# LayerNorm statistics and norms of a chunk: moved from the output stages into K and GLU work

## The chip, the cores and the metric

The kernel runs on one core of one Trainium2 chip. The metric is the device time of one execution in microseconds (us); of several executions the median is given.

## What is computed

The input x has 2048 rows of 640. It is normalised by row and goes through sliding-window attention (32 heads of 20, window 256). A gated unit (GLU) works on the same rows beside it, and x itself is the residual. The core of the reference:

```python
x = A_x
xn = _layernorm(x, axis=-1)
return x + _A_ref(xn, A_wqkv, A_wo) + _B_ref(xn, B_w_gate, B_w_up, B_w_down)

# _A_ref: q, k, v = split(xn @ wqkv); softmax over the last 256 keys; o @ wo
# _B_ref: h = _sigmoid(xn @ w_gate) * (xn @ w_up); h @ w_down
# _layernorm: (x - mean) / sqrt(var + 1e-5)
```

So both branches read the same normalised xn. (B_x is passed in but not used.)

## The kernel before

**Tiling.** The 2048 rows are four chunks of 512 (c = 0 to 3), each of four blocks of 128 rows (s = 0 to 3). Every chunk goes through these stages: LayerNorm with a transpose of the result (xnT, features on partitions), the projections Q and K (`g_qk`, ten blocks of five matmuls), V (`g_v`), the gate and up products of the GLU (`g_gu`, twelve f with a gate half and an up half each), attention, and the output stage (`g_out`: for each block of rows the down product, then Wo into the same PSUM, then the residual).

**LayerNorm of a block.** `ln_block` puts two statistics instructions (L195) and an aggregate (L197) on VectorE (DVE), then two tiny instructions on GpSimd (POOL, L199 and L200), which make rstd out of the variance. `norm_block` (L205) is one DVE instruction that waits for that rstd. `transpose_block` does five TensorE (PE) transposes into one PSUM slot (L213) and one copy out of it into xnT, by DVE for chunks 1 to 3 (L218).

**Attention.** A group is four heads. `scores` (L382) does one step of a group: PE scores (L388), two exps on ScalarE (ACT, L394) and mask selects on POOL (L399, L403). Each group has three steps. `pv` (L407) multiplies a group's probabilities by V (L414), one step into the next group, and DVE finishes the group (L424 to L434).

**The order of the work.** The program order is written out by hand (`manual_schedule`), and every engine works through its queue in that order. The attention steps are the frame (L523). Between two steps `Fill` issues other work: it holds a list of labelled parts (L499 to L513), each a Python generator that issues some instructions and yields their PE cost in ns. After each step a credit, proportional to the step's width, is spent by pulling from the first part. An output stage is shut until its chunk's attention is done (L522, L532). `mix(a, b, first)` (L469) runs generator a and, from its item number `first` on, pulls one item of b after each item of a.

**Where LayerNorm stands.** Chunk 0 is normalised at the start. LN(1) is mixed into the GLU of chunk 0 from item 8 on ("gu0"), LN(2) into output stage 0 from item 6 on ("out0"), LN(3) into output stage 1 from item 6 on ("out1"). `g_ln` (L269) issues for each s the statistics of block s, the norm of block s-1, and the transposes of block s-2; each is an item of its own.

**Buffers that matter.** One PSUM pool, ps_d, has three slots, shared by the projections, gate and up, the two halves of y in the output stage, and the LayerNorm transposes. A gate slot is freed by the tanh on ACT (L316), an up slot by h on DVE (L324), a Q slot by a DVE cast (L238), a K slot by an ACT cast (L240), a V slot by DVE (L264), the y slots by the residual adds on DVE (L357). The tanh results have two buffers (tp), the probabilities four (pp), the normalised blocks xn four.

Of the kernel before, what the change touches and what calls it, by code (L numbers as in the profile page):

```python
# [18 lines left out]
SBC = CW // P  # L19
# [51 lines left out]
def kernel(  # L71
# [119 lines left out]
    def ln_block(c, s):  # L191
        xs = xc[c][:, s, :]
        stats = lnp.tile([P, 2, nc.vector.BN_STATS_DIM], FP32, name="stats")
        for a in range(2):
            nc.vector.bn_stats(out=stats[:, a, :], in_=xs[:, a * 320:(a + 1) * 320])  # L195
        mv = lnp.tile([P, nc.vector.BN_AGGR_DIM], FP32, name="mv")
        nc.vector.bn_aggr(out=mv, in_=stats)  # L197
        rstd = lnp.tile([P, 1], FP32, name="rstd")
        nc.gpsimd.tensor_scalar(out=rstd, in0=mv[:, 1:2], scalar1=EPS, scalar2=None, op0=ADD)  # L199
        nc.gpsimd.tensor_tensor(out=rstd, in0=rstd, in1=neghalf, op=POW)  # L200
        return mv, rstd

    def norm_block(c, s, mv, rstd):
        xn = lnp.tile([P, D], BF16, name="xn", bufs=4)
        nc.vector.tensor_scalar(out=xn, in0=xc[c][:, s, :], scalar1=mv[:, 0:1],  # L205
                                scalar2=rstd[:, 0:1], op0=SUB, op1=MULT)
        xns[c, s] = xn

    def transpose_block(c, s, act):
        xn = xns.pop((c, s))  # L210
        pt = ps_d.tile([P, DC, P], BF16, name="pt", tag="d")
        for d in range(DC):
            nc.tensor.transpose(pt[:, d, :], xn[:, d * P:(d + 1) * P], ident)  # L213
        dst = xnT[c][:, :, s * P:(s + 1) * P]
        if act:
            nc.scalar.copy(out=dst, in_=pt)
        else:
            nc.vector.tensor_copy(out=dst, in_=pt)  # L218

    def new_xnT(c):  # L220
        xnT[c] = xtp.tile([P, DC, CW], BF16, name="xnT")
# [5 lines left out]
    def proj_block(w, c, m):  # L227


        base = 0 if w == "q" else D  # L230
        ps = ps_d.tile([P, CW], FP32, name="pqk", tag="d")
        for d in range(DC):
            wt = wqkv[:, d, base:base + D].rearrange("p (k m) -> p m k", m=DC)
            nc.tensor.matmul(ps, lhsT=wt[:, m, :], rhs=xnT[c][:, d, :],  # L234
                             start=(d == 0), stop=(d == DC - 1))
        st = stp.tile([P, CW], BF16, name="st")
        if w == "q":
            nc.vector.tensor_copy(out=st, in_=ps)  # L238
        else:
            nc.scalar.copy(out=st, in_=ps)  # L240
        dst = scratch[w, c % 2].rearrange("(h j) s -> h j s", j=32)
        nc.sync.dma_start(out=dst[:, 4 * m:4 * m + 4, :], in_=st)

    def spread(w, c, g0, g1):

        if g0 == 0:
            qk[w, c] = (qp if w == "q" else kp).tile([P, NG, CW], BF16, name=w + "T")
        src = scratch[w, c % 2].rearrange("(g p) s -> p g s", p=P)
        nc.sync.dma_start(out=qk[w, c][:, g0:g1, :], in_=src[:, g0:g1, :])
# [16 lines left out]

    MM = 216

    def g_ln(c):  # L269

        new_xnT(c)
        stat = {}
        for s in range(SBC + 2):
            if s < SBC:
                stat[s] = ln_block(c, s)
                yield 0
            if 0 <= s - 1 < SBC:
                norm_block(c, s - 1, *stat[s - 1])
                yield 0
            if 0 <= s - 2:  # L280
                transpose_block(c, s - 2, False)
                yield 5 * 64

    def g_qk(c):
        for w in "qk":
            for m in range(DC):
                proj_block(w, c, m)
                if w == "k" and m == 1:
                    spread("q", c, 0, NG)
                yield 5 * MM  # L290
        if c == 0:
            spread("k", c, 0, 1)
            spread("k", c, 1, NG)

    def g_v(c):
        for s in range(SBC):
            proj_v(c, s)
            if s == 0:
                spread("k", c, 0, NG)
            yield 10 * 136  # L300
# [4 lines left out]
    def part(w, d, f):  # L305
        k, first = divmod(f * P, FS)
        return w[k][:, d, first:first + P]

    def g_gu(c, f0, f1):
        for f in range(f0, f1):  # L310
            pg = ps_d.tile([P, CW], FP32, name="pg", tag="d")
            for d in range(DC):
                nc.tensor.matmul(pg, lhsT=part(wg, d, f), rhs=xnT[c][:, d, :],  # L313
                                 start=(d == 0), stop=(d == DC - 1))
            th = tp.tile([P, CW], FP32, name="th")
            nc.scalar.activation(out=th, in_=pg, func=TANH, scale=0.5)  # L316
            yield 5 * MM
            pu = ps_d.tile([P, CW], FP32, name="pu", tag="d")
            for d in range(DC):
                nc.tensor.matmul(pu, lhsT=part(wu, d, f), rhs=xnT[c][:, d, :],  # L320
                                 start=(d == 0), stop=(d == DC - 1))
            h = hp.tile([P, CW], BF16, name="h")
            ht[c, f] = h
            nc.vector.scalar_tensor_tensor(out=h, in0=th, scalar=1.0, in1=pu, op0=ADD, op1=MULT)  # L324
            yield 5 * MM
# [4 lines left out]
    def out_psum(kind):  # L330
        if kind == "s":
            t = ps_s.tile([P, 2, CW], FP32, name="y", tag="s")
            return [t[:, 0, 0:HALF], t[:, 1, 0:HALF]]
        return [ps_d.tile([P, CW], FP32, name=f"y{i}", tag="d")[:, 0:HALF] for i in range(2)]

    def down(c, s, ys):
        for hf in range(2):
            for f in range(FC):
                nc.tensor.matmul(ys[hf], lhsT=ht[c, f][:, s * P:(s + 1) * P],  # L339
                                 rhs=wd[:, f, hf * HALF:(hf + 1) * HALF],  # L340
                                 start=(f == 0), stop=False)
                if f == 5:
                    yield 6 * 136
            yield 6 * 136

    def outp(c, s, ys, last=False):
        sb = c * SBC + s
        y = yp.tile([P, D], BF16, name="y_sb")

        def wo_half(hf):  # L350
            for m in range(DC):
                nc.tensor.matmul(ys[hf], lhsT=oc[c, m][:, s * P:(s + 1) * P],  # L352
                                 rhs=wo[:, m, hf * HALF:(hf + 1) * HALF],
                                 start=False, stop=(m == DC - 1))

        def add_half(hf):
            nc.vector.scalar_tensor_tensor(  # L357
                out=y[:, hf * HALF:(hf + 1) * HALF], in0=ys[hf], scalar=0.5,
                in1=xc[c][:, s, hf * HALF:(hf + 1) * HALF], op0=MULT, op1=ADD)

        if last:
            for hf in range(2):
                wo_half(hf)
                add_half(hf)
                cut = slice(hf * HALF, (hf + 1) * HALF)
                (nc.scalar, nc.sync)[hf].dma_start(out=out2[sb * P:(sb + 1) * P, cut], in_=y[:, cut])
        else:
            wo_half(0)
            wo_half(1)
            add_half(0)  # L370
            add_half(1)
            nc.sync.dma_start(out=out2[sb * P:(sb + 1) * P, :], in_=y)
        yield 10 * 136

    def g_out(c):
        for s in range(SBC):
            ys = out_psum("d")
            yield from down(c, s, ys)
            yield from outp(c, s, ys)
# [86 lines left out]
            while label not in self.done and self.parts:  # L466
                self.one()

    def mix(a, b, first):  # L469

        for k, cost in enumerate(a):
            yield cost
            if k >= first:
                yield next(b, 0)
        for cost in b:
            yield cost

    new_xnT(0)
    stat = {0: ln_block(0, 0)}
# [12 lines left out]
    fill = Fill()  # L492
    GU = 10 * MM
    OUT = 4 * 34 * 136
    def later(c):
        load_x(c)
        yield 0

    fill.add("gu0", mix(g_gu(0, 0, 12), g_ln(1), 8), 12 * GU + 1280)  # L499
    fill.add("qk1", g_qk(1), 50 * MM)  # L500
    fill.add("v1", g_v(1), 40 * 136)
    fill.add("gu1a", g_gu(1, 0, 1), 1 * GU)
    fill.add("out0", mix(g_out(0), g_ln(2), 6), OUT + 1280)
    fill.add("x3", later(3), 0)
    fill.add("qk2", g_qk(2), 50 * MM)
    fill.add("v2", g_v(2), 40 * 136)
    fill.add("gu1b", g_gu(1, 1, 12), 11 * GU)
    fill.add("out1", mix(g_out(1), g_ln(3), 6), OUT + 1280)
    fill.add("qk3", g_qk(3), 50 * MM)
    fill.add("v3", g_v(3), 40 * 136)  # L510
    fill.add("gu2", g_gu(2, 0, 12), 12 * GU)
# [27 lines left out]
    c = NCH - 1  # L539
# [46 lines left out]
```

## Time and profile before

| what | value |
|---|---|
| median of 13 executions | 341.14 us (339.21 to 343.83) |
| the profiled execution, own time | 340.45 us |
| its span, first to last instruction | 338.6 us |
| mean TensorE clock granted | 0.995 |
| PE, DVE, ACT, POOL busy | 94%, 48%, 64%, 49% of the span |
| share of PE on the chain that ended last | 83% |
| DMA | 30.89 MB, mean 91 GB/s |

Where the stages lie in the span, by the instructions' start times: GLU of chunk 0 with LN(1) from 34 to 67 us, Q and K of chunk 1 from 67 to 83, V of chunk 1 from 83 to 92, output stage 0 with LN(2) from 96 to 121, Q, K and V of chunk 2 from 121 to 143, GLU of chunk 1 from 143 to 173, output stage 1 with LN(3) from 173 to 203.

How to read the profile: the page first gives each engine's busy time, its share of the span and its number of instructions. Then the span is cut into 40 slices of 8.5 us; a digit is the busy share in tenths, and PEclk the granted TensorE clock in tenths. A line of waits says which engine and line waited for which, then the total in us, how many times, and the longest. A table by stretch has the stretch, its length, for PE, its weight loads, DVE, ACT and POOL the busy us with the number of instructions, then the clock, the DMA share and GB/s. A line in order of time has the start, the length (both us), engine, line, operation, and what it writes and reads.

### The profile page before, as it was taken

The page shows a single profiled execution, that of the slowest core. Times are in us where ns is not written, and L with a number is a line of the kernel's source. Part 1 is how long each engine was busy: PE and PEld are TensorE (multiplying, and loading weights), DVE is VectorE, ACT ScalarE, POOL GpSimd, SP SyncE. Part 2 cuts the span into 40 slices and gives each one's busy share as a digit, 9 for nine tenths or more (in the row PEclk, how much of TensorE's full clock was granted, in tenths as well). Part 3 has the DMA queues.
Part 4 walks back from the last instruction along what each step waited for, and adds up shares of the span by engine and source line. Part 5 has one row for each costly group of instructions (what it writes and reads, how often), then busy time and mean ns, then how long its engine had stood idle before and what let it go on. Part 6 is the DMA issues. An engine that isn't in the chain of part 4 may idle for free.

```text
span 338.6 us, 7191 instructions
## 1 busy us (share of the span) xinstructions
PE 318.7 (94%) x2855; PEld 165.8 (49%) x2884; DVE 162.9 (48%) x333; ACT 218.2 (64%) x274; POOL 165.3 (49%) x312
## 2 busy tenths in 40 slices
PE   5999978989899999999999899999999999999996
PEld 2654423435456655544455554544445664444664
DVE  4332079572646853734445846364443434444142
ACT  2623775869675668788874636878787666887300
POOL 5200447554557745564545755545545455554300
PEclk9999999999999999999999979999999999999999
DMA  8947997124600144610000002540000010000002
GB/s 270 376 156 195 360 390 226 38 77 124 205 0 22 41 128 114 221 42 3 0 2 21 19 21 83 181 162 2 2 0 3 21 40 20 2 0 2 2 10 68
DMA packets 26224, 30.89 MB, mean 91 GB/s; under 512 B 1456, under 2 KB 25648, under 8 KB 26160
## 3 DMA queue, kind: packets, MB, share of 16 engines
q1 hardware_dynamic: 25904, 30.20, 27.2%
q8 instruction: 22, 0.36, 0.5%
q10 hardware_dynamic: 288, 0.25, 0.2%
q14 instruction: 10, 0.08, 0.1%
HBM read 21.00 MB, written 10.26 MB: 92 GB/s over the span
## 4 chain that ended last, share of the span: by engine, by line
PE 83%; DVE 6%; ACT 4%; DMA 4%; issue 2%; POOL 1%; SPq 0%; ACTq 0%; POOLq 0%
PE pg L313 14%; PE pu L320 14%; PE y L339 13%; PE pqk L234 13%; PE ps L388 9%; PE acc L414 6%; PE pv L260 6%; PE y L352 6%; ACT pT L394 3%; DMA xc<-in_A_x_dram 2%; DMA sk<-st 1%; DVE stats L195 1%; PE pt L213 1%; DVE t L424 1%; DVE on L430 1%
## 5 line engine op out<-in xcount | busy, mean ns | idle before, releaser
L394 ACT ACTIVATE pT<-ps 128x1024 bf16<-128x1024 f32 (+2 forms) x192 | 175.9, 971 | 66.5 <-PE ps L388 65.0
L399 POOL TENSOR_SCALAR_AFFINE_SELECT pT<-pT 128x512 bf16<-128x512 bf16 x128 | 81.6, 638 | 80.4 <-ACT pT L394 80.4
L403 POOL TENSOR_SCALAR_AFFINE_SELECT pT<-pT 128x512 bf16<-128x512 bf16 x112 | 71.9, 642 | 58.7 <-ACT pT L394 58.7
L324 DVE SCALAR_TENSOR_TENSOR h<-th,pu 128x512 bf16<-128x512 f32 x48 | 32.8, 684 | 62.3 <-ACT pT L394 24.4
L320 PE MATMUL pu<-xnT,wu 128*128 128x512 bf16 x231 | 58.0, 380 | 2.2 <-issue 1.0
L313 PE MATMUL pg<-xnT,wg 128*128 128x512 bf16 x228 | 59.2, 380 | 0.8
L339 PE MATMUL y<-wd,h 128*128 128x320 bf16 x384 | 58.4, 303 | 1.3 <-DVE y_sb L357 1.3
L234 PE MATMUL pqk<-xnT,wqkv 128*128 128x512 bf16 x192 | 45.8, 382 | 0.5 <-issue 0.2
L339 PEld LDWEIGHTS <-h 128*128 128x128 bf16 x384 | 36.1, 99 | 18.6 <-issue 5.4
L388 PE MATMUL ps<-qT,kT 20*128 20x384 bf16 (+2 forms) x704 | 39.6, 277 | 4.2 <-ACT pT L394 3.1
L424 DVE STREAM_TRANSPOSE t<-acc 128x512 f32<-128x512 f32 x32 | 22.9, 715 | 33.0 <-PE acc L414 32.7
L316 ACT ACTIVATE th<-pg 128x512 f32<-128x512 f32 x48 | 28.8, 600 | 14.1 <-PE pg L313 12.3
L313 PEld LDWEIGHTS <-wg 128*128 128x128 bf16 x240 | 22.1, 98 | 27.0 <-issue 3.2
L320 PEld LDWEIGHTS <-wu 128*128 128x128 bf16 x240 | 21.4, 98 | 28.2 <-issue 6.5
L234 PEld LDWEIGHTS <-wqkv 128*128 128x128 bf16 x200 | 22.3, 119 | 19.3 <-issue 2.9
L388 PEld LDWEIGHTS <-kT 20*128 20x128 bf16 x704 | 12.3, 92 | 35.7 <-issue 34.0
L357 DVE SCALAR_TENSOR_TENSOR y_sb<-y,xc 128x320 bf16<-128x320 f32 x32 | 15.1, 488 | 27.0 <-PE y L352 26.9
L414 PE MATMUL acc<-pT,v 128*32 128x384 bf16 (+2 forms) x704 | 26.0, 277 | 1.9 <-POOL pT L403 1.4
L260 PE MATMUL pv<-wqkv,xnT 128*128 128x320 bf16 x160 | 23.9, 299 | 0.4 <-DVE v L264 0.4
L352 PE MATMUL y<-wo,oc 128*128 128x320 bf16 x160 | 24.1, 299 | 0.0
L414 PEld LDWEIGHTS <-v 128*32 128x32 bf16 x704 | 15.1, 96 | 15.4 <-issue 12.5
L238 DVE CAST st<-pqk 128x512 bf16<-128x512 f32 x20 | 13.8, 691 | 13.7 <-PE pqk L234 12.0
(32 smaller groups left out, 175.1 us busy)
## 6 DMA issues: line engine op xcount, KB each, us to landing
qT<-sq SPq DMA_DIRECT2D x4, 1024.0 KB, 5.9
kT<-sk SPq DMA_DIRECT2D x3, 1024.0 KB, 5.5
sq<-st SPq DMA_DIRECT2D x20, 128.0 KB, 2.1
sk<-st SPq DMA_DIRECT2D x20, 128.0 KB, 2.8
wqkv<-in_A_wqkv_dram SPq DMA_DIRECT2D x3, 800.0 KB, 6.8
out_dram<-y_sb SPq DMA_DIRECT2D x15, 160.0 KB, 1.8
wg<-in_B_w_gate_dram SPq DMA_DIRECT2D x2, 960.0 KB
wu<-in_B_w_up_dram SPq DMA_DIRECT2D x2, 960.0 KB
```

The costliest lines, as they stand in the source:

```text
L234: nc.tensor.matmul(ps, lhsT=wt[:, m, :], rhs=xnT[c][:, d, :], start=(d == 0), stop=(d == DC - 1))
L260: nc.tensor.matmul(ps[:, 0:HALF], lhsT=xnT[c][:, d, s * P:(s + 1) * P], rhs=wqkv[:, d, 2 * D + hf * HALF:2 * D + (hf + 1) * HALF], start=( ...
L313: nc.tensor.matmul(pg, lhsT=part(wg, d, f), rhs=xnT[c][:, d, :], start=(d == 0), stop=(d == DC - 1))
L320: nc.tensor.matmul(pu, lhsT=part(wu, d, f), rhs=xnT[c][:, d, :], start=(d == 0), stop=(d == DC - 1))
L324: nc.vector.scalar_tensor_tensor(out=h, in0=th, scalar=1.0, in1=pu, op0=ADD, op1=MULT)
L339: nc.tensor.matmul(ys[hf], lhsT=ht[c, f][:, s * P:(s + 1) * P], rhs=wd[:, f, hf * HALF:(hf + 1) * HALF], start=(f == 0), stop=False)
L352: nc.tensor.matmul(ys[hf], lhsT=oc[c, m][:, s * P:(s + 1) * P], rhs=wo[:, m, hf * HALF:(hf + 1) * HALF], start=False, stop=(m == DC - 1))
L388: nc.tensor.matmul(pss[i // 2][:, i % 2, col * P:(col + n) * P], lhsT=qk["k", kc][32 * i:32 * i + DH, g, kb * P:(kb + 1) * P], rhs=qk["q", ...
L394: nc.scalar.activation(out=pt[:, 2 * a:2 * a + 2, 0:width * P], in_=pss[a][:, :, 0:width * P], func=EXP, scale=SCALE)
L399: nc.gpsimd.affine_select(out=v, in_=v, pattern=[[0, HG], [1, P]], compare_op=GE, fill=0.0, base=0, channel_multiplier=-1)
L403: nc.gpsimd.affine_select(out=v, in_=v, pattern=[[0, HG], [-1, P]], compare_op=GE, fill=0.0, base=-1, channel_multiplier=1)
L414: nc.tensor.matmul(acc[32 * i:32 * i + 32, q0 * P:(q0 + n) * P], lhsT=v[:, h * VW:h * VW + 32], rhs=pt[:, i, col * P:(col + n) * P], start ...
```

## The change

`g_ln` is split in two. `g_norms` keeps statistics and norms; the norm of block s-2 is now issued after the statistics of block s, where it was s-1. `g_transposes` has the transposes alone. `chain` runs generators one after the other, and `mix` gets a parameter `every`, so that b is pulled only at every so-many-th item of a.

For chunk 1 all stays in the GLU of chunk 0, one item later, and all transposes come after all norms. For chunk 2 the statistics and norms go into Q and K of chunk 1, from item 2 on; for chunk 3 into the GLU of chunk 1, from item 10 on. Output stages 0 and 1 keep only the transposes, at items 1, 4, 7 and 10. The costs told to `Fill` stay the same.

```diff
-    def g_ln(c):
+    def g_norms(c):
 
         new_xnT(c)
         stat = {}
@@
             if s < SBC:
                 stat[s] = ln_block(c, s)
                 yield 0
-            if 0 <= s - 1 < SBC:
-                norm_block(c, s - 1, *stat[s - 1])
+            if s >= 2:
+                norm_block(c, s - 2, *stat[s - 2])
                 yield 0
-            if 0 <= s - 2:
-                transpose_block(c, s - 2, False)
-                yield 5 * 64
+
+    def g_transposes(c):
+        for s in range(SBC):
+            transpose_block(c, s, False)
+            yield 5 * 64
+
+    def chain(*gens):
+        for g in gens:
+            yield from g
@@
-    def mix(a, b, first):
+    def mix(a, b, first, every=1):
 
         for k, cost in enumerate(a):
             yield cost
-            if k >= first:
+            if k >= first and (k - first) % every == 0:
                 yield next(b, 0)
@@
-    fill.add("gu0", mix(g_gu(0, 0, 12), g_ln(1), 8), 12 * GU + 1280)
-    fill.add("qk1", g_qk(1), 50 * MM)
+    fill.add("gu0", mix(g_gu(0, 0, 12), chain(g_norms(1), g_transposes(1)), 9), 12 * GU + 1280)
+    fill.add("qk1", mix(g_qk(1), g_norms(2), 2), 50 * MM)
@@
-    fill.add("out0", mix(g_out(0), g_ln(2), 6), OUT + 1280)
+    fill.add("out0", mix(g_out(0), g_transposes(2), 1, 3), OUT + 1280)
@@
-    fill.add("gu1b", g_gu(1, 1, 12), 11 * GU)
-    fill.add("out1", mix(g_out(1), g_ln(3), 6), OUT + 1280)
+    fill.add("gu1b", mix(g_gu(1, 1, 12), g_norms(3), 10), 11 * GU)
+    fill.add("out1", mix(g_out(1), g_transposes(3), 1, 3), OUT + 1280)
```

## The prediction

> **What bounds the kernel now.** I read the page first: engine totals, then the slices.
>
> ```profile
> PE 318.7 (94%) x2855; PEld 165.8 (49%) x2884; DVE 162.9 (48%) x333; ACT 218.2 (64%) x274; POOL 165.3 (49%) x312
> ...
> PE   5999978989899999999999899999999999999996
> ...
> PEclk9999999999999999999999979999999999999999
> ```
>
> TensorE is busy in 318.7 of 338.6 us; no other engine passes 64%. The change leaves PE's work alone, so it can win only PE idle time (19.9 us, head and tail included) and slow PE time (the 7 in PEclk, a slice of 8.5 us). So I asked for busy time by stretch: LN(1) waiting and catching up, the rest of GLU chunk 0, the stage out0, the stage out1, and a short stretch inside out1.
>
> ```profile
> 42.00:54.00 12.00, 7.82 (x72) 3.20 (x65) 9.06 (x23) 6.92 (x10) 6.70 (x13) 1.00 0.95 348
> 54.00:68.00 14.00, 13.84 (x124) 6.25 (x124) 9.59 (x19) 11.63 (x18) 8.74 (x16) 1.00 0.39 106
> ...
> 94.00:122.00 28.00, 27.41 (x298) 17.00 (x297) 18.18 (x41) 17.61 (x19) 19.03 (x35) 1.00 0.05 19
> ...
> 174.00:203.00 29.00, 26.76 (x288) 16.40 (x285) 14.94 (x37) 15.87 (x17) 16.73 (x30) 0.94 0.05 18
> 195.00:199.00 4.00, 3.98 (x26) 2.13 (x26) 1.12 (x3) 1.94 (x2) 2.19 (x4) 0.57 0.12 41
> ```
>
> The first number after the length is PE's busy time. PE misses 4.2 us in 42-54, 0.2 in 54-68, 0.6 in out0, 2.2 in out1; and in 195-199 its clock is 0.57. Then the waits of PE in out1, and DVE in order of time just before.
>
> ```profile
> PE y L339 <- DVE y_sb L357: 1.3, 1, 1.3
> PE pt L213 <- DVE xnT L218: 0.6, 1, 0.6
> PE ps L388 <- ACT pT L394: 0.2, 1, 0.2
> ```
>
> ```profile
> 192.74 0.48 DVE L218 COPY xnT<-pt 128x640 bf16<-128x640 bf16 x1
> 193.14 0.87 DVE L195 BATCH_NORM_STATS2 stats<-xc 128x6 f32<-128x320 bf16 x2
> 194.05 0.21 DVE L197 BATCH_NORM_AGGREGATE mv<-stats 128x2 f32<-128x12 f32 x1
> 194.17 0.39 DVE L205 TENSOR_SCALAR xn<-xc,mv,rstd 128x640 bf16<-128x640 bf16 x1
> 194.48 0.88 DVE L357 SCALAR_TENSOR_TENSOR y_sb<-y,xc 128x320 bf16<-128x320 f32 x2
> ```
>
> The residual adds (L357) that free the next block's PSUM stand behind a copy, statistics and a norm on DVE. Wo had ended at about 192.2; the adds start at 194.48, so down (L339) starts at 195.02.
>
> For GLU chunk 0 the waits of PE in 42-68 read:
>
> ```profile
> PE acc L414 <- POOL pT L403: 1.4, 1, 1.4
> PE ps L388 <- ACT pT L394: 1.1, 2, 0.6
> PE pu L320 <- DVE h L324: 0.8, 1, 0.8
> ```
>
> The cause is in the waits of DVE: its statistics wait 7.5 us for x(1), until 44.48, with h (L324) behind them; POOL's rstd waits 3.8 us for mv with the mask selects behind it.
>
> [...] after the gaps of 0.64 and 1.31 us the clock is 0.50 from 196 to 198; but 42-54, with 4.2 us missing, stays at 1.00. [...] In this trace norms take 0.39 to 0.74 us and selects 0.63 to 0.89[...].
>
> **The change, part by part.** No instruction is added or removed: per chunk 8 statistics (mean 477 ns), 4 aggregates (209), 4 norms (484), and on POOL 4 pairs of rstd (281 + 585). One ln_block is about 1.16 us of DVE; a chunk's move is 4 x 1.16 + 4 x 0.48 = 6.6 us of DVE and 4 x 0.87 = 3.5 us of POOL. No DMA is moved. I placed each step by counting the costs the generators yield against Fill's credit; for the kernel before this gives the trace's order.
>
> (1) *out1 loses LN(3)'s statistics and norms.* The gaps 0.64 and 1.31 go: adds and copies then find DVE with 14.9 - 6.6 = 8.3 us of work in 29. The slow spell behind them should go too. Its price: from 195.02 to 198.93 PE did 6 down, scores, 6 down, a transpose. In out0 at full clock the same steps take 0.91 + 0.33 + 0.82 + 0.28 = 2.34 us by start-to-start, here 3.91: loss 1.57. Together 3.52; without the spell, 1.95.
>
> (2) *out0 loses LN(2)'s.* Its DVE wait (0.35, a transpose behind the copy before) goes: 0.35. The transposes now stand after the 2nd, 5th, 8th and 11th step of the out stage, at least three steps apart (one step is 0.8 us or more), so a third PSUM slot beside y0 and y1 is copied out before it is wanted. Bounds of this part 0.1 to 0.6 (all idle of the stage).
>
> (3) *Chunk 1 in GLU.* Statistics start one step later, behind h of f=4, and norms two blocks behind. x(1) still lands at 44.4. I walk DVE on from there with the trace's durations: two statistics to 46.7, h to 47.4, the finish of group 0 to 49.1, third statistics to 50.2. The 0.77 us PE wait for h and the 1.68 us ACT wait for it go. POOL's third rstd to 51.1, then three selects to 53.0, so the second pv ends near 53.5 where it ended at 53.93. But one more GLU half (1.08 us) is done ahead of it and a transpose (0.28) not yet. By the next pv the lead is smaller: scores S8 are issued at 55.0 to 55.5 against 55.27, exps and selects take 4 us from there, pv at about 59.2 against 60.01, with one transpose more to do. Gain 0.5 to 0.9; I take 0.7, bounds -0.5 (PE waits for DVE, which is full until 57.5) and 1.8 (the lead at 53.5 kept).
>
> (4) *LN(2) into the K/Q stage, 71.4-83.5.* DVE is busy 5.53 of 12.10; with 6.6 it is full. The queue waits behind it: q casts (L238), then the group's transpose (L424). The walk: casts q3, q4 end at 73.7 and 75.5, the group's transpose starts at 75.5 in place of 74.44, all late by about 1.1. Covers: three PSUM slots, and K casts are on ACT. The next PE step needing such a slot is at 76.2. Cost 0; uncovered 1.1.
>
> (5) *LN(3) into GLU chunk 1, 157.3-169.5.* DVE 4.87 + 6.6 of 12.2. Worst in the walk: h of f=7 ends at 165.1 where it ended at 163.9; the tanh that needs its th buffer comes at 166.16: 1.06 us left. POOL 7.42 + 3.5 of 12.2; the first norm runs 6.7 us after its statistics, while the longest lag from mv to rstd in out0 was 107.14 - 102.78 = 4.36. Cost 0, up to 1.2 if the buffers don't cover.
>
> Sum: 3.52 + 0.35 + 0.7 = 4.57 with the spell, 3.0 without. Against the profiled execution (340.45 us, span 338.6): 335.9. What is late next is PE itself: the chain is 83% PE. The median of 13 is 341.14, 0.7 above it. [...] I give it 7 in 10 of the executions: gain 3.0 + 0.7 x 1.57 = 4.1, so **337.0**.
>
> **Rivals.** *A, a slow spell elsewhere (0.20).* In (3) PE's wait before the second pv grows from 1.39 + 0.24 to about 2.3 us in one piece, as it comes to it earlier. If the clock falls there, 1.57 is given back: 338.6, and 339.3 if (3) also gives nothing. For it: PE idled less than that before 195. Against: 42-54 kept its clock.
>
> *B, slower (0.12): the stall moves along.* In (4) and (5) DVE is full, and a norm waiting for rstd would hold h and casts as it held the adds. If each stage got the same stall and spell (2 x 3.52 = 7.0) the result is 337.0 + 7.0 = 344.0. It decides from 2.05 us of PE loss in each, which is 1.06 of cover plus 2.05: DVE about 3.1 us later than in my walk. For: full DVE. Against: the 6.7 us lag.
>
> *C, nothing gained (0.06):* the freed time turns into waits for exp (PE waits 3.1 us for ACT in all now): 340.9. Against: ACT is busy 15.87 of 29 in out1. That the order isn't what the code says is small, since the count matches the trace.
>
> **Numbers.** Forecast 0.62, its own range 335.3 (3.5 + 0.6 + 1.8 gained) to 338.4. About 0.3%, 1.0 us, is what a measurement of this kernel can tell. A is faster by more than that; C within; B slower; from the forecast I leave 0.03 within: faster 0.78, same 0.09, slower 0.13. The range goes from 335.2 to 340.2, through A and the bounds of (2) to (5).
>
> **What would show it.** Right: in out1 no PE wait for y_sb or xnT, clock 1.00 through the stage; the wait of DVE for rstd (5.6 us in all) mostly gone; PE's wait for h gone near 46. Wrong: PE waits for h, th or casts in the K/Q stage of chunk 1 or late GLU of chunk 1; a slice of PEclk below 9 elsewhere; selects late for a pv because rstd stands before them.

## The result and the profile after

The changed kernel takes 335.72 us in the median of 11 executions (334.33 to 338.75), the kernel before beside them 340.62 (48 executions, 338.03 to 344.61). The ratio is 0.9868, interval 0.9843 to 0.9892: 1.3% faster, some 4.5 us (3.7 to 5.3). Forecast were 4.1 us and 337.0, counted from 341.14. Executions more than 1.5% longer than the fastest of their kernel are left out of the ratios here and of the table of clocks below.

The profiled execution of the changed kernel took 338.75 us, the longest of its eleven, only 1.7 less than that of before. So the page's spans can't be compared directly. These are its lines for the engines, the slices and the clock:

```profile
PE 319.3 (95%) x2855; PEld 166.1 (49%) x2884; DVE 163.4 (48%) x333; ACT 218.4 (65%) x274; POOL 165.0 (49%) x312
...
PE   5899878998899999999999999999999999999996
...
PEclk9699999999999999999999999999999999999999
```

The 7 late in PEclk (output stage 1) is gone, but there is a 6 in the second slice, before any code that the change touches. The prediction named a digit below 9 elsewhere as a sign of being wrong; the profiles of e3, e4 and e8 have a slow clock in the head too and others don't, so I don't lay it to the change. To set such accidents apart I cut each profile at the first matmul of each stage. Lengths in us:

| stage | before | before, second profile (e1) | changed |
|---|---|---|---|
| head, up to the gate of f=3 | 33.85 | 33.09 | 37.15 |
| GLU of chunk 0, with LN(1) | 33.42 | 33.53 | 32.43 |
| Q, K, V of chunk 1 | 28.72 | 28.71 | 28.68 |
| output stage 0 | 25.33 | 25.33 | 24.62 |
| Q, K, V of chunk 2, GLU of chunk 1 | 52.11 | 52.11 | 52.10 |
| output stage 1 | 29.98 | 28.41 | 26.78 |
| the rest | 135.19 | 135.22 | 135.24 |

The stages repeat to 0.1 us, the head doesn't. Without the head, and against the second profile, which has no slow clock, the change gains 1.1 + 0.0 + 0.7 + 0.0 + 1.6 = 3.4 us; both stages that took the work over stayed as long as they were.

The table by stretch of the changed kernel (GLU of chunk 0, Q/K/V of chunk 1, output stage 0, output stage 1) shows the work moved and PE fuller:

```profile
37.15:69.58 32.43, 29.19 (x243) 12.23 (x243) 18.33 (x41) 24.07 (x35) 18.11 (x33) 1.00 0.79 264
69.58:98.26 28.68, 26.51 (x236) 13.03 (x237) 22.32 (x49) 21.49 (x30) 18.94 (x41) 1.00 0.40 120
98.26:122.88 24.62, 24.62 (x271) 15.81 (x269) 11.17 (x24) 15.51 (x16) 13.06 (x22) 1.00 0.07 22
174.98:201.76 26.78, 26.01 (x300) 16.50 (x293) 10.45 (x23) 16.68 (x18) 13.29 (x22) 1.00 0.06 20
```

In output stage 0 PE has no idle time left. DVE (third busy number) has 10.45 us in output stage 1. In order of time, DVE around the third block's adds in output stage 1:

```profile
193.00 0.48 DVE L218 COPY xnT<-pt 128x640 bf16<-128x640 bf16 x1
195.03 0.49 DVE L363 SCALAR_TENSOR_TENSOR y_sb<-y,xc 128x320 bf16<-128x320 f32 x1 [1.55 <-PE y L358]
195.71 0.49 DVE L363 SCALAR_TENSOR_TENSOR y_sb<-y,xc 128x320 bf16<-128x320 f32 x1 [0.19 <-PE y L358]
```

Now DVE waits for Wo, where Wo's result waited for DVE. DVE's wait for rstd over the whole kernel fell from 5.6 to 0.9 us. The only PE wait left in this stage is for exp, and it grew from 0.2 us:

```profile
PE ps L394 <- ACT pT L400: 0.8, 2, 0.6
```

### The profile page after: what moved, and what is told of

Same layout as the page of the kernel before. It is cut to its first block, busy times and chain, and to the rows that moved or that the text cites. A ratio compares the mean times of both kernels' runs of the same rounds, so it can differ in the third digit from the quotient of the medians.

```text
span 337.0 us, 7190 instructions
## 1 busy us (share of the span) xinstructions
PE 319.3 (95%) x2855; PEld 166.1 (49%) x2884; DVE 163.4 (48%) x333; ACT 218.4 (65%) x274; POOL 165.0 (49%) x312
## 4 chain that ended last, share of the span: by engine, by line
PE 83%; DMA 7%; ACT 3%; DVE 3%; issue 1%; POOL 1%; SPq 1%; ACTq 0%; POOLq 0%
PE y L345 15%; PE pqk L234 13%; PE pg L319 12%; PE pu L326 12%; PE ps L394 8%; PE pv L260 7%; PE y L358 7%; PE acc L420 6%; DMA xc<-in_A_x_dram 5%; ACT pT L400 3%; PE pt L213 1%; DMA sk<-st 1%; DVE stats L195 1%; DVE t L430 0%; POOL pT L405 0%
## 5 line engine op out<-in xcount | busy, mean ns | idle before, releaser
L345 PE MATMUL y<-wd,h 128*128 128x320 bf16 x384 | 57.3, 300 | 0.0
L260 PE MATMUL pv<-wqkv,xnT 128*128 128x320 bf16 x160 | 26.0, 316 | 0.4 <-DVE v L264 0.4
```

What stands on the lines that cost most here:

```text
L260: nc.tensor.matmul(ps[:, 0:HALF], lhsT=xnT[c][:, d, s * P:(s + 1) * P], rhs=wqkv[:, d, 2 * D + hf * HALF:2 * D + (hf + 1) * HALF], start=( ...
```

## Experiments

**e1: the kernel before, once more.** No edit.

> The kernel before, unchanged, profiled a second time. My theory: the waits of TensorE in output stage 1 (0.64 and 1.31 us) come from the program order and show again to 0.2 us, and the GLU stage of chunk 0 from its third-last half block takes 33.4 us again; the half-clock spell behind the waits (1.57 us lost) [...] it may be there or not. Rival: the whole loss of output stage 1 is an accident of one execution; then the stage takes under 28 us here.

338.21 us in its one execution. PE's waits in output stage 1 (first fence) and the clock in the four us after them (second; PE busy first, clock third from the end):

```profile
PE y L339 <- DVE y_sb L357: 1.3, 1, 1.3
PE pt L213 <- DVE xnT L218: 0.6, 1, 0.6
PE ps L388 <- ACT pT L394: 0.2, 1, 0.2
```

```profile
195.00:199.00 4.00, 4.00 (x51) 2.60 (x52) 1.44 (x4) 1.94 (x2) 2.75 (x6) 1.00 0.13 45
```

The waits are there to the digit, the spell (the stretch at half clock) isn't: 28.41 us in place of 29.98, so the spell costs 1.57. The rival (an accident of one execution) falls for the waits; for the spell it holds.

**e2, e3, e4: one chunk at a time.** Each is the kernel before with the change for one chunk:

```diff
-    fill.add("gu1b", g_gu(1, 1, 12), 11 * GU)
-    fill.add("out1", mix(g_out(1), g_ln(3), 6), OUT + 1280)
+    fill.add("gu1b", mix(g_gu(1, 1, 12), g_norms(3), 10), 11 * GU)
+    fill.add("out1", mix(g_out(1), g_transposes(3), 1, 3), OUT + 1280)
```

and so for chunk 2 (e3: "qk1" and "out0") and chunk 1 (e4: "gu0").

> Only LN(3) is moved, as in the change; LN(1) and LN(2) stand as before. My theory (the adds on VectorE stood behind LayerNorm work): output stage 1 gets shorter by 3.2 us, GLU of chunk 1 doesn't get longer, and the time falls by 2.0 to 3.2 us (0.6 to 0.9%), the largest part of the whole 1.3%. Rival (the gain is the later statistics of chunk 1 in GLU chunk 0): under 1 us.

> Only LN(2) is moved. My theory: output stage 0 gets shorter by 0.5 to 0.7 us, the K and Q stage of chunk 1 stays within 0.1 us, the time falls by some 0.6 us, too little to be clear. Rival (full VectorE in the K and Q stage stalls TensorE): that stage gets longer by up to 1.1 us and the time doesn't fall.

> Only LN(1) is changed: statistics one item later in the GLU of chunk 0, norms two behind, transposes after all. My theory: this stage gets shorter by 1.0 us, the time falls by 0.5 to 1.0 us. Rival (the late x(1) sets the pace whatever the order): within 0.3 us of before.

| kernel | ratio to before (interval) | stage it changes |
|---|---|---|
| e2, LN(3) only | 0.9913 (0.9881 to 0.9944) | output stage 1: 26.78 |
| e3, LN(2) only | 0.9959 (0.9932 to 0.9985) | output stage 0: 24.62 |
| e4, LN(1) only | 0.9927 (0.9900 to 0.9954) | GLU of chunk 0: 32.42 |

Each stage has the length of the full change, and the stages that take the work over have the old length (52.10 in e2, 28.72 in e3). So the three parts are separate and each gains; the rivals of e2, e3 and e4 fall. e2's stage is 3.2 us shorter than the first profile of before, as expected, but half of that is the spell. The times are another matter. e4 got 2.5 us faster (1.6 to 3.4), where I expected 0.5 to 1.0 and its stage gives 1.0; e3 got 1.4 for some 0.6. The three falls add to 2.0% where the whole change has 1.3%. The stages add up and the times don't, so I read the parts from the stages.

The spell strikes elsewhere too: e4's profile has it after the same waits (30.07 us; clock 0.62 from 197.5 to 201.5), e3's doesn't (28.41), and in e2 it fell in the GLU of chunk 0 (34.73 us, where before has 33.4 to 33.5; clock 0.89 from 45 to 60).

**What the executions say of the clock.** Each execution lists its mean granted clock. It comes in steps of about 0.005; over some 338 us one step is 1.7 us of lost clock, about one spell. Executions by number of steps below 1.000, with their median time:

| kernel | 0 | 1 | 2 | 3 |
|---|---|---|---|---|
| before (beside e1 to e4) | 1: 338.37 | 12: 339.70 | 31: 341.35 | 2: 342.91 |
| e2, LN(3) only | 7: 336.95 | 4: 338.09 | 2: 340.14 | 3: 340.49 |
| e3, LN(2) only | 3: 337.59 | 8: 338.84 | 7: 340.77 | 2: 340.31 |
| e4, LN(1) only | 4: 337.04 | 9: 338.69 | 5: 340.68 | none |
| changed | 7: 334.88 | 4: 336.83 | 1: 338.75 | none |

The mean is 1.7 steps before, 1.1 in e2 and e4, 1.4 in e3 and 0.5 changed. (The changed kernel has twelve clocks on record, one more than its median is taken from; the 48 executions of before beside it have none, so the two rows come from different occasions.) In the column without steps the change is worth 3.5 us against before's one such execution, 3.3 against e1: what the stages say. In the column of one step it is 2.9. So the median gains twice: some 3.3 us of waits, and fewer spells. The steps don't say where a spell was, and the head has them as well (the 6 in the slices above), so how many go with each wait is not settled.

The kernels of e5 to e8, e10 and e11 ran once each (336.52, 336.55, 334.35, 339.48, 333.06 and 337.42 us); from them I read the stages alone.

**e5: is it the transposes' places?** The changed kernel with the old places of the transposes:

```diff
-    fill.add("out1", mix(g_out(1), g_transposes(3), 1, 3), OUT + 1280)
+    fill.add("out1", mix_at(g_out(1), g_transposes(3), (11, 14, 16, 17)), OUT + 1280)
```

and the same in "out0"; `mix_at` pulls b at the listed items.

> The changed kernel, but the four transposes of output stages 0 and 1 stand at items 11, 14, 16 and 17, where the kernel before had them, instead of 1, 4, 7 and 10. My theory (it was the LayerNorm work on VectorE ahead of the residual adds, not how close the transposes stand): output stage 0 takes 24.6 to 25.0 us and output stage 1 26.4 to 27.2, as with the change. Rival (the transposes needed spacing, since they share a PSUM slot with y): output stage 1 takes 28 us or more.

Output stage 0 takes 24.97, output stage 1 27.22 us. The rival (28 or more) falls, but the places aren't free: 0.35 and 0.44 us of the gains of 0.71 and 1.63 belong to them. The profile names no wait for them, but the scores show where they lie. From the first score matmul of a step to the next instruction it is 0.33 us as a rule. In output stage 0 two of these steps take 0.48 and 0.55 in e5 (from 110.69 and 116.84), none with the change. In output stage 1 the steps together take 1.75 us above that rule in e5 and 1.33 with the change. So the transposes' places act on how closely the score steps follow each other; why is not shown.

**e6: only the lag.** The kernel before with norms two and transposes three blocks behind, nothing moved to another stage (by the count of items the transposes stay within one item of their old places in the output stages):

```diff
-        for s in range(SBC + 2):
+        for s in range(SBC + 3):
...
-            if 0 <= s - 1 < SBC:
-                norm_block(c, s - 1, *stat[s - 1])
+            if 0 <= s - 2 < SBC:
+                norm_block(c, s - 2, *stat[s - 2])
                 yield 0
-            if 0 <= s - 2:
-                transpose_block(c, s - 2, False)
+            if 0 <= s - 3:
+                transpose_block(c, s - 3, False)
```

> The kernel before, everything in its old stages, but norms two blocks and transposes three blocks behind. My theory is that what counts is what stands on VectorE just ahead of the adds of the third block: here the fourth statistics come earlier and no norm waits for GpSimd, so output stage 1 takes 27.0 to 27.8 us where 28.4 is the length without a clock spell. Rival (it is the sum of VectorE work in the stage): 28.4 or more.

Output stage 1 takes 27.21 us. The table by stretch for this stage:

```profile
171.20:198.50 27.30, 26.42 (x297) 16.17 (x296) 15.31 (x37) 16.07 (x18) 17.40 (x32) 1.00 0.06 19
```

DVE still does 15.31 us in the stage (10.45 with the change), and PE still gets 1.2 of the 1.63 us back. A copy and two norms still stand ahead of the adds (from 190.31, the adds at 191.52), but no statistics. The order just ahead of the adds is what counted, not the sum. PE's wait for the adds shrank from 1.3 to 0.2:

```profile
PE y L360 <- DVE y_sb L378: 0.2, 1, 0.2
```

Output stage 0 stays at 25.34 with the lag: there the moving was needed. In the GLU of chunk 0 the lag alone brings most of the gain (22.04 us after the landing of x(1), see e9).

**e7: norms one block behind.** The changed kernel with `s - 1` again in `g_norms`.

> The changed kernel with norms one block behind again (in K and Q of chunk 1 and in GLU of chunk 1, and in GLU of chunk 0). My theory (the longer lag covers GpSimd's delay): VectorE waits 1.5 to 2.5 us for rstd at the first norm of chunk 3, h of f=7 comes after 166.2 us of the old time base, and the stretch Q2 to the end of GLU 1 gets 0.5 to 1.5 us longer than 52.10. Rival (buffers cover it anyway): 52.1.

52.11 us: no cost. VectorE waited 0.6 us in that stretch, at the fourth norm, not 1.5 to 2.5 at the first: there the finish of group 6 (two transposes, reciprocal, products) stood ahead of the norm and took the time. My expectation fails, the rival holds. In the new stages the longer lag isn't needed.

**e8: how much cover is left.** The changed kernel, in `ln_block`:

```diff
+        if c >= 2:
+            for a in range(2):
+                nc.vector.bn_stats(out=stats[:, a, :], in_=xs[:, a * 320:(a + 1) * 320])
```

> The changed kernel with every statistics instruction of chunks 2 and 3 issued twice, 3.8 us more on VectorE in each of the two stages that took the work over (the first result is overwritten by the second). It measures what cover is left. My theory: VectorE then has some 15 us of work in 12 us, so the stretch with GLU of chunk 1 gets 1 to 2.5 us longer, and the Q, K and V stretch of chunk 1 0 to 2 us. Rival (much cover left): both within 0.1 us of 52.10 and 28.68.

Q, K, V of chunk 1 take 29.26 (0.58 more), Q2 to the end of GLU 1 52.96 (0.86 more), and output stage 1 26.35 (0.43 less). PE's one wait in the late part is at the stage's end, for an h that stands behind the finish of a group:

```profile
PE y L348 <- DVE h L333: 0.8, 1, 0.8
```

So 3.8 us more on VectorE cost 0.6 in the first stretch and 0.9 in the second, of which output stage 1 gives 0.4 back. Most of the 3.8 us was still covered, not all; where between 0 and 3.8 us the cover ends, this run doesn't say. My 1 to 2.5 was high for the second, and the rival falls.

**e9, e10: what sets the GLU of chunk 0.** Set x(1)'s landing (when the first statistics start) beside the stage's length, both from the gate of f=3 on:

| profile | landing | stage | difference |
|---|---|---|---|
| before | 10.63 | 33.42 | 22.79 |
| e1, before | 10.72 | 33.53 | 22.81 |
| e3, old order | 10.48 | 33.27 | 22.79 |
| changed | 10.61 | 32.43 | 21.82 |
| e4, new order | 10.60 | 32.42 | 21.82 |
| e5, new order | 11.51 | 33.33 | 21.82 |
| e8, new order | 11.36 | 33.18 | 21.82 |

In these seven the end follows the landing to 0.02 us. The other three profiles so far fit less well than the expectation of e9 says: e7 has 21.87, e6 has 22.04 (the lag in the old place), and e2, with a spell in this stage, 24.26. So neither e6's early start nor e7's short lag costs much by itself; which part of the new order brings the 0.98 is not isolated. e9 puts `load_x(1)` ahead of the loop over `load_gu(k)` in `load_rest`; e10 has 11 in place of 9 in "gu0".

> The changed kernel with the load of x(1) put ahead of the loads of the second halves of the gate and up weights. In all ten profiles so far the GLU stage of chunk 0 ends 21.8 us (new order) or 22.8 us (old order) after x(1) lands, whatever the landing, so I take its landing to set the pace. My theory: x(1) lands some 5 us earlier (1920 KB at 370 GB/s), the statistics never wait, the stage gets shorter by 1.0 to 2.0 us and the time with it. Rival (the weights that now come later are wanted at f=6, and TensorE waits for them instead): same or longer.

> The changed kernel with LN(1) from item 11 on instead of 9 in the GLU of chunk 0. My theory (fewer of VectorE's h instructions stand behind the statistics that wait for x(1)): the stage gets shorter by 0.3 to 1.0 us than 21.8 us after the landing. Rival (the transposes then come so late that the projections wait for the last copy): no gain, TensorE waiting for xnT at the first projection.

| kernel | stage | result |
|---|---|---|
| e9 | 30.47 us | 333.78 us median of 6, ratio to before 0.9794 (0.9762 to 0.9827) |
| e10 | 30.65 us, landing 10.62 | 333.06 us in one execution |

In e9 the statistics start at 39.28 with no wait for the load. PE's waits in its GLU of chunk 0 hold none for h, and none for the weights:

```profile
PE ps L394 <- ACT pT L400: 1.4, 3, 0.6
PE ps L394 <- DMA kT<-sk: 1.1, 1, 1.1
PE pu L326 <- issue: 0.2, 1, 0.2
```

Both rivals fall. e9 gains 2.1% on the kernel before (clock included), its stage 1.96 us on the changed kernel. e10 gains 1.8 us in the same stage, more than the 0.3 to 1.0 I had expected; PE has no wait for h there. By the sum of stages e9 is 0.3 us shorter than e10.

**e11: the stall put back.** The changed kernel, in `outp` between Wo and the adds (results unused):

```diff
             wo_half(1)
+            if (c, s) == (1, 2):
+                junk = lnp.tile([P, 2, nc.vector.BN_STATS_DIM], FP32, name="stats")
+                for a in range(8):
+                    nc.vector.bn_stats(out=junk[:, 0, :], in_=ys[1])
             add_half(0)
```

> The changed kernel with eight statistics instructions (of the PSUM half y1, results unused) put on VectorE between Wo and the residual adds of the third block in output stage 1, 3.9 us in all. It puts back only what I hold for the cause of the old stall. My theory: down of the fourth block waits 1 to 2 us for the adds, the stage takes 1 to 2 us more than 26.78, and if the clock falls after it, 1.57 more. Rival (the old stall had another cause, the adds have slack): 26.8.

Output stage 1 takes 29.58 us, 2.80 more. The fence has what stood on VectorE, and the next PE's wait:

```profile
191.49 4.23 DVE L379 BATCH_NORM_STATS2 stats<-y 128x6 f32<-128x320 f32 x8 [2.22 <-PE y L358]
195.64 0.87 DVE L363 SCALAR_TENSOR_TENSOR y_sb<-y,xc 128x320 bf16<-128x320 f32 x2
```

```profile
PE y L345 <- DVE y_sb L363: 2.6, 1, 2.6
```

Work ahead of the adds alone makes the stall; the rival falls. The instructions took 4.23 us, and the stall is longer than my 1 to 2. The clock did not fall after it: PEclk is 9 in all 40 slices.

## Why the prediction was right, step by step

(1) **Output stage 1**: the mechanism was right. The waits went, but of the 1.95 us forecast 1.63 came (28.41 to 26.78). PE's wait for exp rose by 0.6 (0.7 in e5): two score steps now follow each other with a transpose and only six down matmuls between them. That leaves some 1.2, which is what e5 has; the transposes' places add 0.44, not foreseen either. Nor was it foreseen that the lag alone brings 1.2 of it (e6). The spell was priced right (1.57) and its frequency was a guess of mine: I gave it 7 in 10; after this stall it showed in two of four profiles (before and e4; not e1 and e3). What decides it is not shown.

(2) **Output stage 0**: the term was mis-sized, 0.71 for 0.35, and outside my bound of 0.6, all the idle time the profile showed. Half of it (0.36, e5) is the work that left, half (0.35) the transposes' new places, where PE was counted as busy. Idle time is no upper bound where the work is put in another order.

(3) **GLU of chunk 0**: 0.99 by the pairs above for 0.7. The walk had the right direction and the wrong limit: I let POOL's selects hold up the second pv and expected 2.3 us of PE waiting there; the trace has 0.2. The wait for h, which was to go, moved and grew, from 0.8 to 1.26 us (0.57 and 0.69). So that the size came near is in part luck. The stage hangs on the landing of x(1), 21.82 us after it in place of 22.80.

(4), (5) **The stages that took the work over** cost 0, as forecast (28.72 to 28.68; 52.11 to 52.10). e8 shows the limit: 3.8 us more does cost. The reason I gave with (5), a lag that must cover GpSimd's 4.36 us delay, isn't needed (e7).

Sum: 3.3 us of waits for my 3.0, with errors of -0.3, +0.4 and +0.3 that partly cancel. Of the 4.5 measured this leaves some 1.2 for fewer spells, for my 1.1; the table of clocks would give 2.1 (1.2 steps of 1.7 us), so this part is known only roughly. Two slips in the forecast's sums change nothing: its range starts at 335.3 in one place and 335.2 in another, and its chances give 0.79 faster and 0.12 slower, not 0.78 and 0.13. **Rival A** rested on a long wait before the second pv, which didn't come. **Rival B** (the stall moves along) is wrong here; e8 shows where it would begin. **Rival C** has a trace of truth, the 0.6 us of exp waits in (1).

## What to carry to other kernels

Look at what stands on an engine just ahead of the instruction that frees TensorE's PSUM: moving that within the stage brought 1.2 of 1.63 us here (e6), with VectorE's work in the stage as before (15.31 us, 15.16 in e1). Cut profiles by stage before comparing them, and set each execution's granted clock beside its time: here that separates 3.3 us of waits from what the clock adds. If a stage ends at a fixed time after a load lands (here 21.82 us), load earlier or start the work later; e9 and e10 got 1.96 and 1.8 us in that stage from this, the reordering 0.98.

## What the hardware showed that I had not expected

In two of four profiles (before, e4) the clock stood at half for 3.41 us after PE's waits of 0.64 and 1.31 us; in the other two (e1, e3) it stayed at 1.00 after the same waits, and in e11 after one wait of 2.65 us. In the head of the changed kernel it stood at half for 6.83 us, from 8.04 to 14.87. Here are stretches of 3.41 to 3.42 us, with PE's busy time after the length and the clock third from the end: of before, the one ahead of the fall and the one at half clock; of e4, the one ahead of the fall.

```profile
192.06:195.48 3.42, 1.47 (x19) 0.87 (x18) 3.39 (x10) 1.94 (x2) 1.38 (x4) 1.00 0.00 0
195.48:198.89 3.41, 3.41 (x23) 1.68 (x22) 0.64 (x2) 1.86 (x2) 1.72 (x3) 0.50 0.14 48
195.04:198.46 3.42, 1.80 (x20) 1.03 (x20) 3.12 (x9) 1.73 (x2) 1.95 (x4) 1.00 0.04 14
```

So PE was idle for 1.95 us of the stretch ahead of the fall in before, and for 1.62 in e4. But e1 has 1.96 us of waits between 191.96 and 194.36, and e11 its 2.65 us in one piece, and there the clock stayed. It stayed too in 42-54 of before, where 4.2 us of 12 are missing. Between 30 and 320 us the thirteen traces have three falls: these two, and the one of e2 in the GLU of chunk 0. So neither the longest wait nor the idle time within some 3.4 us tells by itself whether the clock falls; what does is not shown.
